# RWKV6 attention and MLP-mixer on one core: another order of the same pieces on the engines

## The chip, the core and the metric

The kernel runs on one core of a Trainium2 chip. The core has five engines with queues of their own: PE (matrix products), DVE and ACT (elementwise work, copies, scans), POOL (elementwise work) and SP, which here only issues DMAs. The 16 DMA engines of the core move data between DRAM and the on-chip memory. Products are summed in PSUM, of which this kernel hands out banks of 128 partitions x 512 numbers. The metric is the device time of one execution in microseconds; lower is better. Before the change three runs took 478.63, 479.74 (the median) and 480.80 us.

## The reference

Four sequences (B = 4) of 768 tokens, 8 heads of 48 numbers. The attention carries a 48 x 48 state for each head from token to token; the mixer then works on the 384 joined numbers of each token, first across tokens (768 to 256 to 768), then across channels (384 to 1536 to 384).

```python
for t in range(S):
    kt, vt, rt, wt = (k[:, :, t], v[:, :, t], r[:, :, t], w[:, :, t])
    cur = np.einsum('bhd,bhe->bhde', u[None] * kt, vt)
    y[:, :, t] = np.einsum('bhd,bhde->bhe', rt, state + cur)
    state = wt[:, :, :, None] * state + np.einsum('bhd,bhe->bhde', kt, vt)
...
x = y.transpose(0, 2, 1, 3).reshape(B, S, H * D)
xt = x.transpose(0, 2, 1)
h = np.maximum(xt @ w_tok1, 0.0) @ w_tok2
u = x + h.transpose(0, 2, 1)
h2 = np.maximum(u @ w_ch1, 0.0) @ w_ch2
return (u + h2).astype(np.float32)
```

## The kernel before

The attention is done in 12 **units** (NU), three to a batch, each 256 tokens of all heads, that is four chunks of T = 64 tokens. Inside a chunk products of keys and queries replace the recurrence; between chunks the state is carried. For a unit i these pieces stand in `attention_pieces(i)`:

- **loads** (`load_rk(i + 1)`, L189): the rows r and k of the *next* unit, four DMAs of 192 KB, keys first. They overwrite a buffer that an earlier unit used.
- **ends** (L452, L456, L457) and **begins** (L464): scans on DVE over the decays w, backwards and forwards. **keys** (L461) and **queries** (L467): DVE scales the rows by them, in place.
- **tokens** (L366): PE turns the scaled keys; **copied** (L371): ACT copies them out of PSUM. **carry** (L386): PE's products of keys and v for the state. **gram** (L336): 64 small products of keys and queries, masked by DVE (L509).
- **scaled** (L522, ACT) and **updates** (L537, DVE): the state chunk by chunk. **before** (L401): products of the queries with the states; **after** (L422): the products within the chunk; **taken** (L428): ACT copies the result into x.
- **w** (L182), **v** (L202), **near** (L207): further loads of the next unit.

A **visit** below means a stretch in which PE takes several of these pieces one behind the other: up to 64 tiny matmuls of 48 or 64 columns in each of before, carry, gram and after.

The mixer is run for each batch. The first batch's (`first_mixing`) has single products: back (L715), turn, up (L964), down (L975), then an add on DVE (L979) into a tile `o`, and its store to the output (L980). The others (`exact_mixing`) add up products of rounded parts ("forms") of both operands: hidden (L684), back (L724), turn (L730), ends and joints (L761 to L768), down (L779 to L781). The forms of the weights are made once, by ACT and DVE (L600 to L622), parts of them are stored to DRAM (L613, L615; tiles `third`), and each of the three later mixings reads these back through a ring of tiles (L647).

**What sets the order.** Each piece is a Python closure that emits instructions for one or more engines. `interleaved(ORDER, ...)` has ten streams of pieces: 0 the products of all mixings, 1 the joints, 2 and 3 the passes that turn the sums into forms for the second products, 4 to 6 the units by i modulo 3, 7 the loads of rows, 8 the conversion and forms of the weights, 9 the second hidden forms. Each digit of the string `ORDER` (L50 to L61) takes the next piece of that stream; 1133 digits in all. `strict()` then ties the instructions on PE, DVE, ACT and SP so that each engine keeps just this order. An engine that meets an instruction whose input isn't there waits, and with it all that is behind. The six PSUM banks are handed out in the order of the table too (`with_banks`). The first 46 us or so, three units of the first batch, stand in a list written by hand ahead of `interleaved`.

Of the kernel before, what the change touches and what calls it, by code (L numbers as in the profile page):

```python
# [47 lines left out]
LEAST, MOST = 2.0 ** -40, 2.0 ** 40  # L48
MID = 3 * G // 4 * SEG1
ORDER = (  # L50
    "888880800080800808008088480884800088040804888000088880448404444848848484880800800888800808040800888444080448888884888800"
    "088888004408474888888080844450588858008850008840000550054588545585845588558454050580555500505508708868800608060608045008"
    "068608566668865656680060688566658668886668908658680608678060888684849606800609488994900840840088000408841401044140440448"
    "008004000000000000040000000044044000000007004040450000000000000004000000005000000005000000000010110055000000005000050004"
    "000500050000000000455547455555555450045555000505600640000000576666666560000000000000000066050006066600066666000666666006"
    "605424655642409062622002020092902329939333340000400044400400001414044100400000400000000000040000000000004444440000000000"
    "740400000500000000000000000050000040500004000010115000500000000005000005500000000050050040455450555055755555055566400006"
    "000506006000660060000054650064000000000065600660606065050066666006600006229666065666202020069220092293939330003230000010"
    "000110000000000000000000000000000000000000000000000000000000000000000000000000000000001001017000000000000000000000000000"
    "00000000000000000000000000000000000000000000000000000"  # L60
)  # L61


# [1248 lines left out]
```

## Time and profile before

| | before |
|---|---|
| median of three runs | 479.74 us (478.63 to 480.80) |
| the profiled execution: time, span | 480.81 us, 479.1 us |
| mean granted clock of PE | 0.995 |
| busy: DVE, ACT, POOL | 338.0, 255.8, 59.8 us |
| moved by DMA | 83.77 MB, 175 GB/s over the span |
| DMA of the rows (L189), issue to landing | median 5.6 us over 36 transfers |

The span is what the profiler recorded from the first to the last instruction; the execution's own time is 1.7 us longer. Three stages follow the hand-written start: the mixing of the first batch with units 3 to 5 of the second (to about 187 us), two mixings beside units 6 to 8 and 9 to 11 (to about 294 and 398 us), and the last mixing. In the views quoted below a row of the timeline has the start and the duration in us, the engine (SPq is a DMA issue on SP), the line, the operation and tiles, how many instructions it joins, and in brackets how long the engine was idle before and for what. A row of the stages has each engine's busy time in that stretch and, in parentheses, its instructions; then the granted clock of PE, the mean busy share of the DMA engines and GB/s.

### The profile page before, as it was taken

The page shows a single profiled execution, that of the slowest core. Times are in us where ns is not written, and L with a number is a line of the kernel's source. Part 1 is how long each engine was busy: PE and PEld are TensorE (multiplying, and loading weights), DVE is VectorE, ACT ScalarE, POOL GpSimd, SP SyncE. Part 2 cuts the span into 40 slices and gives each one's busy share as a digit, 9 for nine tenths or more (in the row PEclk, how much of TensorE's full clock was granted, in tenths as well). Part 3 has the DMA queues.
Part 4 walks back from the last instruction along what each step waited for, and adds up shares of the span by engine and source line. Part 5 has one row for each costly group of instructions (what it writes and reads, how often), then busy time and mean ns, then how long its engine had stood idle before and what let it go on. Part 6 is the DMA issues. An engine that isn't in the chain of part 4 may idle for free.

```text
span 479.1 us, 12687 instructions
## 1 busy us (share of the span) xinstructions
PE 459.6 (96%) x5298; PEld 404.6 (84%) x5298; DVE 338.0 (71%) x478; ACT 255.8 (53%) x588; POOL 59.8 (12%) x58
## 2 busy tenths in 40 slices
PE   3698999999999999999999999999999999999996
PEld 2585588856797668999989979999999979999995
DVE  7999799898787687675588966677596556235341
ACT  6688775765777566341547555251747344033140
POOL 1000000000000001240404001250404003032130
PEclk9989999999999999999999999999999999999999
DMA  8856663765663746764668823394595512336231
GB/s 311 328 187 218 175 214 111 236 217 165 192 185 89 244 144 219 228 190 145 183 219 244 286 79 116 121 269 135 164 262 173 164 49 82 111 106 197 83 101 55
DMA packets 49407, 83.77 MB, mean 175 GB/s; under 512 B 4864, under 2 KB 40576, under 8 KB 49344
## 3 DMA queue, kind: packets, MB, share of 16 engines
q1 hardware_dynamic: 49056, 82.80, 54.8%
q8 instruction: 43, 0.70, 0.6%
q14 instruction: 20, 0.16, 0.1%
q10 hardware_dynamic: 288, 0.10, 0.1%
HBM read 71.87 MB, written 11.01 MB: 173 GB/s over the span
## 4 chain that ended last, share of the span: by engine, by line
PE 92%; DMA 3%; ACT 2%; issue 1%; DVE 1%; SPq 1%; DVEq 0%; ACTq 0%
PE bank L975 10%; PE bank L768 8%; PE bank L761 8%; PE bank L779 8%; PE bank L763 8%; PE bank L781 8%; PE bank L780 8%; PE bank L964 7%; PE bank L684 5%; PE bank L960 3%; PE bank L715 3%; PE bank L336 2%; PE bank L401 2%; PE bank L422 2%; PE kv_ps L386 2%; DMA w<-in_w_dram 2%
## 5 line engine op out<-in xcount | busy, mean ns | idle before, releaser
L754 POOL TENSOR_TENSOR z_high<-z_high 128x384 fp32r<-128x384 f32 x48 | 58.5, 1227 | 403.7 <-DMA ring<-third 187.9
L743 ACT ACTIVATE z_high<-bank 128x384 fp32r<-128x384 f32 x48 | 23.5, 490 | 61.4 <-PE bank L768 61.1
L750 DVE SCALAR_TENSOR_TENSOR z_high<-bank,z_high 128x384 fp32r<-128x384 f32 x48 | 26.4, 553 | 35.0 <-ACT z_high L743 35.0
L522 ACT ACTIVATE before<-state,to_end 112x48 f32<-112x48 f32 x132 | 33.3, 325 | 32.4 <-DVE state L537 20.7
L768 PE MATMUL bank<-z_more,forms 128*128 128x384 f32 x216 | 50.1, 340 | 0.0
L761 PE MATMUL bank<-x_forms,forms 128*128 128x384 f32 x216 | 49.9, 339 | 0.0
L763 PE MATMUL bank<-x_forms,ring 128*128 128x384 f32 x216 | 49.4, 337 | 0.0
L975 PE MATMUL bank<-wch,z 128*128 128x384 f32 x144 | 48.5, 489 | 0.0
L779 PE MATMUL bank<-forms,z_high 128*128 128x384 f32 x140 | 48.2, 344 | 0.0
L787 DVE SCALAR_TENSOR_TENSOR x<-bank,x 128x384 f32<-128x384 f32 x35 | 18.8, 551 | 41.1 <-PE bank L781 41.0
L781 PE MATMUL bank<-forms,z_high 128*128 128x384 f32 x140 | 47.2, 337 | 0.0
L780 PE MATMUL bank<-ring,z_high 128*128 128x384 f32 x140 | 47.1, 337 | 0.0
L975 PEld LDWEIGHTS bank<-wch,z 128*128 128x128 f32 x144 | 26.7, 190 | 17.0
L768 PEld LDWEIGHTS bank<-z_more,forms 128*128 128x128 f32 x216 | 39.0, 188 | 0.0
L761 PEld LDWEIGHTS bank<-x_forms,forms 128*128 128x128 f32 x216 | 38.5, 188 | 0.4
L763 PEld LDWEIGHTS bank<-x_forms,ring 128*128 128x128 f32 x216 | 38.6, 188 | 0.0
L964 PE MATMUL bank<-xT,wch 128*128 128x256 f32 x144 | 31.5, 380 | 0.0
L964 PEld LDWEIGHTS bank<-xT,wch 128*128 128x128 f32 x144 | 27.1, 190 | 3.7
L746 ACT ACTIVATE z_high<-z_high 128x384 fp32r<-128x384 f32 x48 | 25.3, 526 | 3.8 <-ACT z_high L743 0.4
L779 PEld LDWEIGHTS bank<-forms,z_high 128*128 128x128 f32 x140 | 26.3, 188 | 0.3
L780 PEld LDWEIGHTS bank<-ring,z_high 128*128 128x128 f32 x140 | 26.3, 188 | 0.0
L781 PEld LDWEIGHTS bank<-forms,z_high 128*128 128x128 f32 x140 | 26.3, 188 | 0.0
(212 smaller groups left out, 925.6 us busy)
## 6 DMA issues: line engine op xcount, KB each, us to landing
ring<-third SPq DMA_DIRECT2D x144, 192.0 KB, 3.0
raw<-in_w_ch_dram SPq DMA_DIRECT2D x16, 512.0 KB, 4.8
rk<-in_rk_dram SPq DMA_DIRECT2D x36, 192.0 KB, 5.6
near<-in_near_dram SPq DMA_DIRECT2D x8, 768.0 KB, 5.2
w<-in_w_dram SPq DMA_DIRECT2D x10, 520.5 KB, 4.4
vt<-in_v_dram SPq DMA_DIRECT2D x12, 384.0 KB, 4.5
out_dram<-x SPq DMA_DIRECT2D x17, 192.0 KB, 1.9
third<-forms SPq DMA_DIRECT2D x12, 192.0 KB, 3.1
```

Source lines behind the costliest of these rows:

```text
L522: act.mul(t[:ROWS, a], state[bt, g][:ROWS, a], by_last(c, j)[:, a:a + 1])
L746: act.mul(z_form(jt, 2), z_form(jt, 0).bitcast(f32), 1.0 / BASE)
L750: dve.scalar_tensor_tensor(z_form(jt, 1), a, 0.0, z_form(jt, 0).bitcast(f32), op0=ALU.max, op1=ALU.subtract)
L754: pool.tensor_add(z_form(jt, 2), z_form(jt, 2).bitcast(f32), z_form(jt, 1).bitcast(f32))
L761: pe.matmul(a, up[m], xf(0)[:, m], start=m == 0, stop=False)
L763: pe.matmul(a, low[:, m], xf(1)[:, m], start=False, stop=False)
L768: pe.matmul(banks["a", jt], joint, xf(2)[:, m], start=False, stop=m == 2)
L779: pe.matmul(a, z[0], up, start=first, stop=False, skip_group_check=True)
L780: pe.matmul(a, z[1], held[bt, s, half, 1, jt], start=False, stop=False, skip_group_check=True)
L781: pe.matmul(a, z[2], joint, start=False, stop=last, skip_group_check=True)
L964: pe.matmul(ps, now["wch1"][:, m, ts(jt, 128)], xT[:, m, ts(s, SEG)], start=(m == 0), stop=(m == DM // 128 - 1))
L975: pe.matmul(ps, zs[s][:, jt, ts(n, 128)], now["wch2"][:, jt, :], start=(jt == 0), stop=(jt == NJ - 1))
```

## The change

Only the string `ORDER` is replaced. The number of digits of each kind is the same, and within a stream the pieces keep their order, so every engine gets the same instructions with the same operands, in another order between the streams; with it, the PSUM banks fall to other pieces.

```diff
-    "605424655642409062622002020092902329939333340000400044400400001414044100400000400000000000040000000000004444440000000000"
-    "740400000500000000000000000050000040500004000010115000500000000005000005500000000050050040455450555055755555055566400006"
...
+    "966406692296666262422000000440992934332234000332444000700104000110444000000040000000000000000400000044004400400404000000"
+    "000440000400000000000000000005000000000000101010005550000000000000000040005054500500005005545445507550055555555405006400"
```

The first place is SP around the loads of unit 6's rows (`rk_89`, L189 `x4`; the sixth unit uses this buffer), in the first batch's mixing. `out_dram<-o` (L980) are its outputs, `near` is a load of unit 5, `third` parts of the weight forms, `ring` the ring of the next mixing. Before:

```order
L615 DMA third_1_138<-wch_127 128x2x384
L207 DMA near<-in_near_dram 128x1536
L615 DMA third_2_139<-wch_127 128x2x384
L189 DMA rk_89<-in_rk_dram 48x1024 x4
L980 DMA out_dram<-o 128x384 x2
L615 DMA third_3_140<-wch_127 128x2x384
```

and with the change:

```order
L207 DMA near<-in_near_dram 128x1536
L615 DMA third_1_138<-wch_127 128x2x384
L615 DMA third_2_139<-wch_127 128x2x384
L980 DMA out_dram<-o 128x384 x2
L189 DMA rk_89<-in_rk_dram 48x1024 x4
L615 DMA third_3_140<-wch_127 128x2x384
```

The four loads moved from ahead of two output stores to behind them.

The second place is DVE at the same time: the adds that make these outputs (L979), form steps (L604, L619), and unit 6's ends (L452 to L457) and keys (L461). Before:

```order
L604 TENSOR_TENSOR forms_1268<-wch_127,forms_1873 128x768
L979 TENSOR_TENSOR o<-x,bank_884 128x384
L979 TENSOR_TENSOR o<-x,bank_882 128x384
L619 TENSOR_TENSOR forms_1268<-forms_1873,wch_127 128x768
L452 MEMSET starts 112x17
L456 SCALAR_TENSOR_TENSOR to_end_93<-w_90,starts 112x1041
L457 RECIPROCAL starts<-to_end_93 112x16
L461 TENSOR_TENSOR rk_89<-rk_89,to_end_93 112x1024
```

and with the change:

```order
L604 TENSOR_TENSOR forms_1309<-wch_127,forms_1882 128x768
L452 MEMSET starts 112x17
L456 SCALAR_TENSOR_TENSOR to_end_93<-w_90,starts 112x1041
L457 RECIPROCAL starts<-to_end_93 112x16
L979 TENSOR_TENSOR o<-x,bank_886 128x384
L979 TENSOR_TENSOR o<-x,bank_882 128x384
L619 TENSOR_TENSOR forms_1309<-forms_1882,wch_127 128x768
L461 TENSOR_TENSOR rk_89<-rk_89,to_end_93 112x1024
```

The ends moved ahead of both adds. (The scans of L456 and L464 carry the name of the instruction that they are built into; the profile calls them TENSOR_TENSOR_SCAN.)

The third place is SP around the loads of unit 8's rows, at a visit to units 6 and 7 in the second batch's mixing; w, vt and near are other loads of unit 8. Before:

```order
L182 DMA w_90<-in_w_dram 128x1041
L647 DMA ring_2148<-third_4_135 128x384
L189 DMA rk_89<-in_rk_dram 48x1024 x4
L202 DMA vt<-in_v_dram 128x2x384
L207 DMA near<-in_near_dram 128x1536
L647 DMA ring_2024<-third_5_136 128x384 x2
```

and with the change:

```order
L647 DMA ring_2149<-third_4_135 128x384 x2
L182 DMA w_90<-in_w_dram 128x1041
L202 DMA vt<-in_v_dram 128x2x384
L189 DMA rk_89<-in_rk_dram 48x1024 x4
L207 DMA near<-in_near_dram 128x1536
L647 DMA ring_2022<-third_5_136 128x384 x2
```

The rows moved behind vt, which overwrites a tile that unit 6's within-chunk products (L422) read in this visit. On PE the carry of unit 7 (L386) moved ahead of the products of unit 6's queries with the states (L401) in it.

More of the change, by code (lines that the diff above doesn't have):

```diff
@@ L50 @@
 ORDER = (
[L51 to L54, printed above, removed]
@@ L55 @@
-    "000500050000000000455547455555555450045555000505600640000000576666666560000000000000000066050006066600066666000666666006"
-    "605424655642409062622002020092902329939333340000400044400400001414044100400000400000000000040000000000004444440000000000"
-    "740400000500000000000000000050000040500004000010115000500000000005000005500000000050050040455450555055755555055566400006"
-    "000506006000660060000054650064000000000065600660606065050066666006600006229666065666202020069220092293939330003230000010"
@@ L59 @@
-    "000110000000000000000000000000000000000000000000000000000000000000000000000000000000001001017000000000000000000000000000"
-    "00000000000000000000000000000000000000000000000000000"
+    "808888800808800400808084808800080080880044488800488808480008480884888880408884808448080888884804808888400488000484880888"
+    "844440084004444480750000550088888888800005540585880500058885804584584585555458505808055588857058088006080400540066606568"
+    "080860566868668550866666606066086056888686696898860688868455060866798800049408480990488080804488448070044481001100880008"
@@ new lines @@
+    "000000000040000000000400000004400000000440044404000040040004000000000000000000000550000000100011050040000500000000055000"
+    "050005000504500000054544550555055555700554055060404000006005005706006600566060060000000550666060606050666060060566000066"
+    "966406692296666262422000000440992934332234000332444000700104000110444000000040000000000000000400000044004400400404000000"
+    "000440000000400000000000000005000000000000101010005550000000000000000040005054500500005005545445507550055555555405006400"
@@ L61 @@
+    "000606060000000045006000656650000000660656506500066666000066009656660060266600252660200066690022232993923903023030000000"
+    "100110000000000000000000000000000000000000000000000000000000000000000000000000000000000100110000000000000000000000000000"
+    "00000000000000000000000000000000000000000000007000000"
 )
```

## The prediction

> **What bounds the kernel now.** I read the busy times on the page first, then the same by stage, then PE's stretches of 10 us, then PE's waits, and last the timelines around the places that the new table reorders.
>
> ```profile
> PE 459.6 (96%) x5298; PEld 404.6 (84%) x5298; DVE 338.0 (71%) x478; ACT 255.8 (53%) x588; POOL 59.8 (12%) x58
> ```
> ```profile
> core 0: us, PE busy (x) PEld busy (x) DVE busy (x) ACT busy (x) POOL busy (x), PEclk, DMA share, GB/s
> 46.00:60.00 14.00, 13.60 (x50) 8.10 (x51) 10.10 (x14) 10.75 (x16) 0.00 (x0) 1.00 0.68 207
> 60.00:187.00 127.00, 127.00 (x1425) 95.17 (x1424) 106.90 (x137) 84.99 (x180) 0.00 (x0) 1.00 0.57 180
> 187.00:294.00 107.00, 105.88 (x1267) 100.46 (x1266) 78.41 (x117) 53.33 (x132) 20.98 (x16) 1.00 0.63 197
> 294.00:398.00 104.00, 104.00 (x1138) 98.72 (x1137) 70.59 (x110) 49.99 (x125) 21.34 (x16) 1.00 0.52 158
> 398.00:471.00 73.00, 73.00 (x423) 72.93 (x422) 27.50 (x53) 21.59 (x43) 16.21 (x16) 1.00 0.37 112
> ```
> From 60 us to 471 us PE is busy in 127.00 + 105.88 + 104.00 + 73.00 = 409.88 of 411 us, at the full granted clock. The table leaves every piece on PE as it was; it sets only their order. So it cannot shorten what PE does, only the time that PE stands still, and behind the hand-written start (to about 46 us, unchanged) that is 0.40 us in 46 to 60 and 1.12 us in 187 to 294. The waits of PE and its 10-us stretches name the second:
> ```profile
> PE bank L336 <- issue: 1.1, 1, 1.1
> ```
> ```profile
> 230.00:240.00 10.00, 9.75 (x179) 1.00 0.65 180
> 240.00:250.00 10.00, 9.13 (x148) 1.00 0.63 205
> ```
> 0.25 + 0.87 = 1.12 us, one pause. The most that a new order can gain here is therefore 1.1 us, or 1.5 with the 0.40. A measurement of this kernel tells from no change about 0.5%, which is 2.4 us of 479.74: under 477.34 or over 482.14. A gain of that size is out of PE's reach; a loss is not, since any piece that PE, in its fixed order, meets before its input is there costs in full.
>
> **The pause, and what the change does at it (a gain).** PE's timeline at the visit to units 6 and 7:
> ```profile
> 237.53 0.96 PE L401 MATMUL bank<-before,rk 48*64 48x48 f32 x42
> 239.21 0.54 PE L336 MATMUL bank<-rk 48*64 48x64 f32 x21
> 240.87 0.85 PE L336 MATMUL bank<-rk 48*64 48x64 f32 x41 [1.12 <-issue]
> ```
> It stops between two matmuls of one gram, 21 of 62 done, for 1.12 us, and no semaphore is named. What the tiny matmuls of a visit need quickly is instructions: four pieces of up to 64 matmuls, each matmul with its weight load, 42 of them in the first 0.96 us. The DMA views show how they come:
> ```profile
> q8 instruction: 43, 0.70, 0.6%
> ...
> w<-in_w_dram SPq DMA_DIRECT2D x10, 520.5 KB, 4.4
> ```
> ```profile
> DMA packets 496, 1.18 MB, mean 295 GB/s; under 512 B 59, under 2 KB 305, under 8 KB 495
> ...
> q1 hardware_dynamic: 495, 1.17, 97.9%
> q8 instruction: 1, 0.02, 2.3%
> ```
> ```profile
> 232.93 0.32 SPq L647 DMA_DIRECT2D ring<-third  x1
> 233.34 0.39 SPq L182 DMA_DIRECT2D w<-in_w_dram  x1
> 234.49 0.32 SPq L647 DMA_DIRECT2D ring<-third  x1
> 234.86 4.89 SPq L189 DMA_DIRECT2D rk<-in_rk_dram  x4
> ```
> 0.70 MB in 43 packets is 16 KB each. In the whole program PE starts 2 x 5298 matmuls and weight loads, 10596, which is one packet for about 246 of them: a visit eats two. From 234 to 238 the data queue alone held the 16 engines for 97.9%, and one packet ran in there at the end. What filled them is w of unit 8 (520.5 KB), a ring tile (192 KB) and the first two transfers of unit 8's rows (2 x 192 KB): 1.10 MB, close to the 1.17 MB counted. In the new table those rows (L189) stand on SP behind vt of unit 8, and vt can only be overwritten when the within-chunk products (L422) of unit 6 have read it, that is behind the visit. 384 of 1100 KB leave the crush; at the 295 GB/s of the window's row they are 1.3 us of it. So the packet may come up to 1.3 us sooner, and the pause may vanish (1.12 us). Bounds of the gain: nothing, if the packet is late for another reason, and 1.1. I take 0.9, because most of the crush before the packet is gone but w and the ring tiles are still there. The Trainium skill ("Runtime: NRT & Kernel Launch", section "Instruction fetch mechanics") says that instructions come in 16 KiB blocks of 256 over a queue of the engine's own, which the trace bears out (43 packets of 16 KB), and that crossing a block is "mostly hidden". By that sentence the pause would not be a packet and nothing would be gained; the 1.12 us without a semaphore speak against it, and it stands below as rival D.
>
> **Unit 6's rows (a loss).** SP and DVE as they were:
> ```profile
> 159.99 2.41 SPq L189 DMA_DIRECT2D rk<-in_rk_dram  x4
> 165.35 1.66 SPq L980 DMA_DIRECT2D out_dram<-o  x2
> 167.09 6.29 SPq L615 DMA_DIRECT2D third<-wch  x2
> ```
> ```profile
> 162.51 0.96 DVE L604 TENSOR_TENSOR forms<-wch,forms 128x768 fp32r<-128x768 f32 x1 [1.07 <-ACT forms L600]
> ...
> 164.76 0.56 DVE L979 TENSOR_TENSOR o<-x,bank 128x384 f32<-128x384 f32 x1 [1.29 <-PE bank L975]
> 166.05 0.55 DVE L979 TENSOR_TENSOR o<-x,bank 128x384 f32<-128x384 f32 x1 [0.73 <-PE bank L975]
> 167.55 2.33 DVE L456 TENSOR_TENSOR_SCAN to_end<-w,starts 112x1041 f32<-112x1041 f32 x1
> 169.91 0.26 DVE L457 RECIPROCAL starts<-to_end 112x16 f32<-112x16 f32 x1
> 170.08 1.16 DVE L461 TENSOR_TENSOR rk<-rk,to_end 112x1024 f32<-112x1024 f32 x1
> 172.02 2.32 DVE L464 TENSOR_TENSOR_SCAN w<-w,starts 112x1041 f32<-112x1041 f32 x1
> ```
> ```profile
> 163.17 2.85 PE L975 MATMUL bank<-wch,z 128*128 128x384 f32 x8
> 165.95 1.15 PE L422 MATMUL bank<-vt,at 64*64 64x48 f32 x64
> 167.02 7.36 PE L684 MATMUL bank<-x,wtok 128*128 128x384 f32 x22
> 174.22 0.93 PE L366 MATMUL bank<-ident,rk 112*128 112x112 f32 x8
> ```
> The rows were issued at 159.99 and used by DVE at 170.08; the keys were ready at 171.24, 2.98 us before PE turned them (L366) at 174.22. In the new table the four transfers stand behind the two outputs (L980), and SP takes them in order. The outputs wait for their adds on DVE (L979). These wait twice: PE now does the last down-products (L975) behind unit 5's within-chunk products and one hidden product (L684, two matmuls, 7.36 / 11 = 0.67 us), so that they end near 167.75 instead of at 163.17 + 2.85 = 166.02, and DVE now does unit 6's ends (L456, L457) ahead of the adds. My walk along the queues: the form step ahead (L604), one later in its chain than the one quoted, gets its input from ACT near 164.4 and ends near 165.4; ends take 2.33 + 0.26 and a memset, to 168.1; the adds run to 168.6 and 169.1; their outputs go out on SP near 168.65 and 169.15, each with about 0.4 us of issue; the two transfers of keys, which come first of the four, at 169.55 and 169.95. How long they take is the open number:
> ```profile
> L189 SPq DMA_DIRECT2D rk<-in_rk_dram x4: 413/421/423, 195.4 to 196.8; - x4
> ...
> DMA to landing us min/median/max: 3.2/4.5/5.1
> DMA to landing us min/median/max: 5.9/6.0/6.2
> ```
> The first two rows are unit 7's rows, the last unit 6's in the old order, close behind other loads. The new place has the two outputs (384 KB) ahead, and in the old order the engines idled there:
> ```profile
> q1 hardware_dynamic: 336, 0.47, 21.6%
> ```
> That is 168 to 174. So the price lies by the first row: landing after 3.2 to 4.5 us, at 173.2 to 174.5, bounds 173.2 and 176.15 (169.95 + 6.2). The keys take 1.16: ready at 174.4 to 175.7, at the latest 177.3. PE comes to L366 at 174.05 to 174.2 (the same pieces stand ahead of it), so it waits 0.2 to 1.5 us, at most 3.1. I take 0.8. Behind the late keys DVE has the begins (2.32) and a form step (0.94) before the add of the first back-product, whose turn on PE (L730) is three pieces later: another 0.3 us, bounds 0 and 0.5. This place costs 1.1 us (0.2 to 3.6).
>
> **The rest.** The other moves I walked the same way (each queue in its new order, with the durations of the trace): unit 3's ends and keys are earlier, its rows later on SP but in time; the transposes of units 5 and 10, unit 8's products and the banks of the down-products have their input before PE's turn by my walk, though some by only a few tenths; from 385 us on the order is as before. I cost them at nothing. What hides them is the other products that PE has ahead of them; where that cover is short, PE waits out the shortfall, some tenths at such a place. Of the 0.40 us in 46 to 60 I count nothing as won.
>
> **The sum.** The profiled execution took 480.81 us (span 479.1, 1.7 around it), 1.07 above the median 479.74 of the runs shown, 478.63 to 480.8. 480.81 - 0.9 + 1.1 = 481.0 by its own time; by the median 479.74 + 0.2 = 479.9. I name 480.3, between the two and nearer the median, as what is compared is medians.
>
> **The rivals.**
> A, the forecast (0.46): pause gone, rows late by about as much. 479.7 to 481.
> B, pause gone and rows in time (0.19). It needs the keys to land within 3.2 us, as unit 7's fastest did; the 21.6% speak for it. 479.74 - 1.1 = 478.6. It could not be told from no change.
> C, the rows' wait takes over, and it is slower (0.23). One mechanism: SP holds unit 6's rows until the outputs leave, and they land in 5.9 to 6.2 us, as unit 6's did before. PE waits 3.1 us at L366 and 0.5 behind it; with 0.9 won, 479.74 + 2.7 = 482.4. It decides from a landing at about 5.9 us: then 2.4 us net. Against it speaks the empty DMA stretch; for it, that the same rows took 6 us, and that adds 0.3 us late on DVE shift all that follows.
> D, the change doesn't do what it says (0.12): the pause isn't a late packet's, or the packet is as late with the rows gone, since w (520.5 KB) and the ring are still there. Then nothing is won and 1.1 lost: 480.8; with the rows landing late, 483.3.
>
> **How the numbers follow.** Range: B's 478.6 less the runs' half spread would reach 477.6, and C's 482.4 with D's far end 483.3; leaving out a tenth on either side gives 478.3 to 483.0. Faster by over 0.5%: only B with a lucky spread, 0.04. Slower by over 0.5%: two thirds of C (0.16), a third of D (0.04), and 0.06 of A for a place whose slack I have wrong, 0.26. The rest, 0.70, is within 0.5%.
>
> **What would show it.** Right: no wait "issue" of PE at L336 near 240 us, unit 8's L189 issued behind L422 of that visit, PE busy 10.00 there; at 174 us a wait of PE at L366 of 0.2 to 1.5 us for DVE L461, itself waiting for the DMA of rk issued behind L980 near 169.6. Wrong: PE's pause still there with the rows gone (D); L461 starting by 173 (B), or after 175.8 (C); or a wait of PE of over 0.5 us at any other line between 60 and 385 us, which none of my walks gives.

## The result, and the profile after

The changed kernel takes 481.48 us (median of 22 runs, 479.57 to 482.91), the kernel before, on the same chips, 479.55 (22 runs). The ratio is 1.0038, 95% interval 1.0026 to 1.0051: slower by some 1.2 to 2.4 us, a small loss that the runs do tell from nothing, within the bound of 0.5% or at its edge. The profiled execution of the changed kernel took 480.78 us with a span of 479.0 us, 0.7 under its median; that of the kernel before had 480.81, 1.26 over its own. The two spans are therefore alike by chance, and the time has to be looked for stage by stage.

The busy times on the page of the changed kernel, and its stages (columns as before):

```profile
PE 460.9 (96%) x5298; PEld 404.9 (85%) x5298; DVE 340.2 (71%) x478; ACT 254.9 (53%) x588; POOL 56.4 (12%) x58
```
```profile
core 0: us, PE busy (x) PEld busy (x) DVE busy (x) ACT busy (x) POOL busy (x), PEclk, DMA share, GB/s
46.00:60.00 14.00, 13.91 (x54) 8.53 (x53) 11.76 (x17) 11.54 (x17) 0.00 (x0) 1.00 0.75 248
60.00:187.00 127.00, 126.39 (x1420) 93.89 (x1419) 105.83 (x134) 83.34 (x175) 0.00 (x0) 1.00 0.59 178
187.00:294.00 107.00, 107.00 (x1274) 101.64 (x1273) 79.94 (x118) 53.29 (x132) 18.82 (x16) 1.00 0.66 202
294.00:398.00 104.00, 103.05 (x1131) 97.73 (x1130) 71.26 (x109) 50.41 (x127) 20.12 (x16) 1.00 0.48 151
```

Where PE was full before (60 to 187, 294 to 398) it now stands still for 0.61 and 0.95 us, and where it had stood still (187 to 294) it is full. PE's waits between 46 and 470 us in the changed kernel (what it waited for, us in total, times, longest):

```profile
PE bank L336 <- issue: 0.9, 1, 0.9
PE bank L366 <- DVE rk L461: 0.6, 1, 0.6
```

The second is the wait that was forecast. The first reads like the one of before, but it is another: it stands 106 us later. PE's timeline at the visit to units 6 and 7, and then at that to units 9 and 10:

```profile
238.32 0.92 PE L401 MATMUL bank<-before,rk 48*64 48x48 f32 x42
239.20 1.26 PE L336 MATMUL bank<-rk 48*64 48x64 f32 x60
240.25 1.14 PE L422 MATMUL bank<-vt,at 64*64 64x48 f32 x64
...
345.37 0.52 PE L336 MATMUL bank<-rk 48*64 48x64 f32 x17
346.84 0.85 PE L336 MATMUL bank<-rk 48*64 48x64 f32 x42 [0.95 <-issue]
```

The pause near 240 us is gone; an equal one has come up in the next visit of this shape. What leads there on SP, first in the kernel before, then in the changed one:

```profile
335.79 6.98 SPq L647 DMA_DIRECT2D ring<-third  x6
342.86 1.96 SPq L182 DMA_DIRECT2D w<-in_w_dram  x1
```
```profile
332.47 9.02 SPq L647 DMA_DIRECT2D ring<-third  x6
341.58 0.38 SPq L182 DMA_DIRECT2D w<-in_w_dram  x1
```

The load of w for unit 11 (520.5 KB) leaves SP 1.3 us sooner. It used to be issued so late that its data ran behind PE's packet of instructions; now they run ahead of it. Its 128 rows of 4,164 bytes started from 345.44 us on in the kernel before, where PE's packet had started at 343.04; in the changed one they started between 342.69 and 344.49, and the packet at 344.35.

Unit 6's rows on SP, DVE and PE in the changed kernel, with the landing of the four loads:

```profile
167.31 0.83 SPq L980 DMA_DIRECT2D out_dram<-o  x2
168.19 1.84 SPq L189 DMA_DIRECT2D rk<-in_rk_dram  x4
```
```profile
DMA to landing us min/median/max: 3.1/4.1/4.8
```
```profile
166.62 0.26 DVE L457 RECIPROCAL starts<-to_end 112x16 f32<-112x16 f32 x1
166.79 0.95 DVE L979 TENSOR_TENSOR o<-x,bank 128x384 f32<-128x384 f32 x2
167.66 0.95 DVE L619 TENSOR_TENSOR forms<-forms,wch 128x768 fp32r<-128x768 f32 x1
172.53 1.23 DVE L461 TENSOR_TENSOR rk<-rk,to_end 112x1024 f32<-112x1024 f32 x1 [3.92 <-DMA rk<-in_rk_dram]
```
```profile
166.61 6.61 PE L684 MATMUL bank<-x,wtok 128*128 128x384 f32 x20
173.81 0.99 PE L366 MATMUL bank<-ident,rk 112*128 112x112 f32 x8 [0.59 <-DVE rk L461]
```

Each step stands as the prediction had it: ends, adds, stores, rows, a wait of 3.92 us on DVE for them, then one of 0.59 us on PE for the keys.

### The profile page after: what moved, and what is told of

Its sections match the earlier page's. It is cut to its first block, busy times and chain, and to the rows that moved or that the text cites. A ratio compares the mean times of both kernels' runs of the same rounds, so it can differ in the third digit from the quotient of the medians.

```text
span 479.0 us, 12698 instructions
## 1 busy us (share of the span) xinstructions
PE 460.9 (96%) x5298; PEld 404.9 (85%) x5298; DVE 340.2 (71%) x478; ACT 254.9 (53%) x588; POOL 56.4 (12%) x58
## 4 chain that ended last, share of the span: by engine, by line
PE 90%; DVE 3%; DMA 3%; ACT 2%; issue 1%; SPq 0%; DVEq 0%; ACTq 0%
PE bank L975 10%; PE bank L768 8%; PE bank L761 8%; PE bank L779 8%; PE bank L763 8%; PE bank L781 8%; PE bank L780 8%; PE bank L964 7%; PE bank L684 4%; PE bank L960 3%; PE bank L715 3%; PE bank L336 2%; PE bank L401 2%; PE bank L422 2%; PE kv_ps L386 2%; PE bank L724 2%
## 5 line engine op out<-in xcount | busy, mean ns | idle before, releaser
L754 POOL TENSOR_TENSOR z_high<-z_high 128x384 fp32r<-128x384 f32 x48 | 55.2, 1161 | 407.4 <-DVE z_high L750 196.7
L761 PE MATMUL bank<-x_forms,forms 128*128 128x384 f32 x216 | 49.9, 339 | 0.0
L780 PE MATMUL bank<-ring,z_high 128*128 128x384 f32 x140 | 47.1, 337 | 0.0
L761 PEld LDWEIGHTS bank<-x_forms,forms 128*128 128x128 f32 x216 | 38.5, 188 | 0.4
L964 PE MATMUL bank<-xT,wch 128*128 128x256 f32 x144 | 31.7, 380 | 0.0
L780 PEld LDWEIGHTS bank<-ring,z_high 128*128 128x128 f32 x140 | 26.3, 188 | 0.1
## 6 DMA issues: line engine op xcount, KB each, us to landing
w<-in_w_dram SPq DMA_DIRECT2D x10, 520.5 KB, 4.5
```

What stands on the lines that cost most here:

```text
L754: pool.tensor_add(z_form(jt, 2), z_form(jt, 2).bitcast(f32), z_form(jt, 1).bitcast(f32))
L761: pe.matmul(a, up[m], xf(0)[:, m], start=m == 0, stop=False)
L780: pe.matmul(a, z[1], held[bt, s, half, 1, jt], start=False, stop=False, skip_group_check=True)
L964: pe.matmul(ps, now["wch1"][:, m, ts(jt, 128)], xT[:, m, ts(s, SEG)], start=(m == 0), stop=(m == DM // 128 - 1))
```

## The experiments

Two runs are of the unaltered kernels; seven are of one of the two tables with one or two pieces of SP moved and nothing else; three have a wait of SP as well. The move is made in the list of pieces that the table yields, by a pair (piece, the piece behind which it goes):

```diff
+MOVED = (((5, 'loads'), (5, 'seen')), ((10, 'w'), (10, 'v')))
...
-        out = [with_banks(*next(left_of[int(n)])) for n in order]
-        return out
+        taken = {p[0]: p for p in (next(left_of[int(n)]) for n in order)}
+        keys = moved(list(taken), MOVED)
+        return [with_banks(*taken[key]) for key in keys]
```

`moved` takes each first piece out and puts it in again right behind the second. "(5, 'loads')" loads the rows of unit 6, "(10, 'w')" the w of unit 11. Each ratio below is to the kernel before on the same chip.

To read them without the chance of single executions, one table for all, from the starts of PE's matmuls in each profile: the time from the first turn of the first batch (L940) to the last product of L715, near 52 and 397 us; three pieces of that stretch; and two gaps between successive matmuls. Column A goes from the first hidden product of the second batch (the first L684) to the first L761, near 158 to 185 us, and holds unit 6's rows. B goes on from there to the 47th product of L780, near 185 to 245 us, and holds the visit to units 6 and 7. C, from the 73rd to the 144th product of L761, near 294 to 366 us, holds the visit to units 9 and 10. A gap is taken from one start to the next, so it is longer than the wait in the views (1.34 against 1.12 us in the kernel before). The gap at 45 us lies in the hand-written start, ahead of the stretch.

| kernel | stretch | A | B | C | gap in B | gap in C | gap at 45 us | ratio |
|---|---|---|---|---|---|---|---|---|
| before | 343.15 | 28.03 | 59.94 | 72.55 | 1.34 | 0.00 | 1.77 | |
| b_again | 343.07 | 28.03 | 59.66 | 72.52 | 1.06 | 0.00 | 0.02 | |
| b_rows8_late | 341.97 | 28.04 | 58.56 | 72.52 | 0.00 | 0.00 | 0.25 | 0.9991 |
| b_rows8_more | 342.22 | 28.04 | 58.58 | 72.52 | 0.00 | 0.00 | 1.25 | 0.9984 |
| b_rows6_late | 344.04 | 29.21 | 59.38 | 72.52 | 0.78 | 0.00 | 0.67 | 1.0033 |
| b_w11_early | 343.03 | 28.03 | 58.79 | 73.37 | 0.21 | 0.71 | 1.39 | 1.0008 |
| changed | 344.35 | 26.63 | 58.69 | 73.79 | 0.05 | 1.16 | 0.32 | 1.0038 |
| a_again | 344.64 | 26.68 | 58.98 | 73.76 | 0.37 | 1.14 | 1.68 | |
| a_rows6_early | 343.42 | 25.45 | 58.72 | 74.03 | 0.07 | 1.40 | 0.32 | 1.0003 |
| a_w11_late | 345.46 | 26.49 | 58.97 | 74.77 | 0.32 | 0.00 | 0.32 | 1.0013 |
| a_both | 342.69 | 25.45 | 59.40 | 72.58 | 0.78 | 0.00 | 0.32 | 0.9997 |
| a_fixed | 342.29 | 25.45 | 58.99 | 72.62 | 0.36 | 0.00 | 0.32 | 0.9989 |
| a_fixed_start | 342.65 | 25.45 | 59.31 | 72.59 | 0.68 | 0.00 | 0.32 | 0.9982 |
| b_best | 341.97 | 28.04 | 58.56 | 72.52 | 0.00 | 0.00 | 0.32 | 0.9960 |

(In A the two tables put different products between its ends, so that only kernels of one table are compared there. At 45 us a matmul of that line takes 0.32 by itself.)

**b_again: the kernel before, once more.**

> The kernel before, unaltered, profiled once more. Theory (a pause of PE is a packet of instructions that comes late behind data): the pause of 1.1 us at L336 near 240 us comes back, since unit 8's rows fill the DMA engines ahead of its packet in every execution; the pause of 1.3 us at L918 near 45 us, in the hand-written start that the change leaves alone, was chance of that one execution and is gone or shorter. Rival (both are fixed waits of the program): both come back within 0.1 us.

One run, 479.25 us. The pause near 240 us is there, 0.8 us by the waits; that at 45 us isn't (0.02). So the first has a standing cause, though its size moves, and the second comes and goes. The execution profiled at first was unlucky in a part that the change leaves alone, and that is why the two spans agreed.

**b_rows8_late and b_rows8_more: only the rows of unit 8 behind the visit.**

```diff
+MOVED = (((7, 'loads'), (7, 'v')),)
```

> The kernel before with one move on SP: unit 8's rows behind unit 8's vt, as in the change. Theory: the pause at L336 near 240 us is gone (0.1 us or less) and nothing else alters, 0.9 to 1.2 us faster, ratio 0.9975 to 0.9982. Rival (the pause belongs to the visit, or to carry standing behind before on PE): the pause stays at 1.1 us, ratio 1.000.

> The kernel before with unit 8's rows behind unit 8's vt, once more, for a narrower interval beside b_best on the same chip. Theory: no pause near 240 us, ratio 0.9975 to 0.9995. Rival: a pause of 0.5 us or more there in this execution, ratio 1.000.

0.9991 (0.9978 to 1.0005) and 0.9984 (0.9964 to 1.0005). The first lies over the range that was expected for it, and the times alone don't settle it, since both intervals take in 1. The profiles do: no gap at the place in either, B 1.1 to 1.4 us shorter than in the two profiles of the kernel before, A and C the same within 0.03 us. In the old table this move alone is worth what that part of the change was thought to be. One smaller pause, 0.2 us, stands at the visit near 152 us in the second.

**b_rows6_late: only the rows of unit 6 behind the output stores.**

```diff
+MOVED = (((5, 'loads'), ('down', 2, 1, 10)),)
```

> The kernel before with one move on SP: unit 6's rows behind the two output stores, as in the change, but DVE and PE in the old order, so that the stores leave near 165.4 and 166.6 us. Theory: rows issued from about 167 us, landing 3.1 to 4.8 later; the keys start near 171 instead of 170.1, PE still has about 2 us left at L366: no wait, ratio 1.000 within 0.001. The cost in the change would then need DVE's and PE's new order as well. Rival (the move on SP alone costs what the change lost there): PE waits 0.5 us or more at L366, ratio 1.001 to 1.002.

1.0033 (1.002 to 1.0046), and A 1.18 us longer. The theory's "no wait" was wrong. The rival had the loss, but not its place, and 1.0033 lies over the 1.002 that it allowed. DVE, ACT and PE in this kernel:

```profile
170.91 1.23 DVE L461 TENSOR_TENSOR rk<-rk,to_end 112x1024 f32<-112x1024 f32 x1 [2.19 <-DMA rk<-in_rk_dram]
172.05 0.95 DVE L604 TENSOR_TENSOR forms<-wch,forms 128x768 fp32r<-128x768 f32 x1
```
```profile
173.03 0.84 ACT L607 ACTIVATE wch<-forms 128x768 f32<-128x768 f32 x1 [2.78 <-DVE forms L604]
173.78 0.85 ACT L686 ACTIVATE h<-bank 128x384 f32<-128x384 f32 x2
```
```profile
172.77 0.93 PE L366 MATMUL bank<-ident,rk 112*128 112x112 f32 x8
174.69 2.85 PE L724 MATMUL bank<-h,wtok 128*128 128x384 f32 x8 [0.98 <-ACT h L686]
```

The keys were ready in time for L366, as expected. But DVE waited 2.19 us for the rows, and behind the keys in its queue stood a form step (L604); ACT waited for that form (L607), and behind it in ACT's queue stood the copies of the hidden products (L686), for which PE waited 0.98 us at L724. The late rows cost PE a microsecond over two queues that have nothing to do with them. The reserve at the piece that reads the rows (from their being ready to their use), 2.98 us before, was the wrong one to read.

**b_w11_early: w of unit 11 ahead of the last ring load.**

```diff
+MOVED = (((10, 'w'), (2, ('ends', 1, 4))),)
```

> The kernel before with one move on SP: w of unit 11 ahead of the last ring load before the visit to units 9 and 10 instead of behind it, so that it is issued near 341.3 us instead of 342.9, as in the change. Theory: its data run when PE's packet is asked for, the packet starts 0.5 to 1.3 us later than before and a pause of 0.3 to 1.2 us appears at L336 near 346 us, 1.0006 to 1.0025. Rival (the new pause comes from the new order on PE, the carry ahead of the products with the states): no pause there, ratio 1.000.

1.0008 (0.9982 to 1.0034): 1 and the whole range of the theory lie in the interval, so the times can't tell. The profile can. SP, and PE at the place:

```profile
340.68 0.38 SPq L182 DMA_DIRECT2D w<-in_w_dram  x1
341.85 0.32 SPq L647 DMA_DIRECT2D ring<-third  x1
```
```profile
345.03 0.64 PE L336 MATMUL bank<-rk 48*64 48x64 f32 x28
346.17 0.73 PE L336 MATMUL bank<-rk 48*64 48x64 f32 x33 [0.50 <-issue]
```

In none of the six other profiles of the old table is there a gap here; with that one move, and PE's order as before, there is one of 0.71. Here the rows of w started between 341.76 and 343.78 us, and PE's packet at 343.94. So the new pause comes from where w stands on SP, and the carry ahead of the products with the states isn't needed for it. That the pause in B was only 0.21 in this execution shows again how its size moves.

**a_again: the changed kernel, once more.**

> The changed kernel, unaltered, profiled once more. Theory: PE waits 0.5 to 0.8 us at L366 near 173 us for unit 6's keys, pauses 0.8 to 1.2 us at L336 near 346 us with no semaphore named, and not near 240 us. Rival (the pauses fall where they will): one of them is missing, or another of 0.5 us stands elsewhere behind 60 us.

One run, 483.12 us. L366 waits 0.6 us, the pause in C is there (1.14), that in B is a third of what it was (0.37), and the one at 45 us struck here (1.68).

**a_rows6_early: the rows of unit 6 ahead of the stores again.**

```diff
+MOVED = (((5, 'loads'), (5, 'seen')),)
```

> The changed kernel with one move on SP: unit 6's rows ahead of the two output stores again. Theory: the keys are done before 170 us, the wait at L366 is gone and with it what followed on DVE, 0.7 to 1.2 us less than the change, ratio to the kernel before 1.0013 to 1.0024 where the change has 1.0038. Rival (the rows weren't what PE waited for there, DVE's order was): the wait stays at 0.5 us or more, ratio 1.0033 to 1.0043.

1.0003 (0.9985 to 1.0021), still lower than the theory's 1.0013, which its interval takes in. The wait at L366 is gone, A is 1.18 us shorter (0.81 of it up to the first L724, 0.37 behind it), and the pause in C stays, as nothing was done about it.

**a_w11_late, a_both and a_fixed: w of unit 11 behind the visit, alone and with the former; then held by a wait.**

```diff
+MOVED = (((10, 'w'), (10, 'v')),)
...
+MOVED = (((5, 'loads'), (5, 'seen')), ((10, 'w'), (10, 'v')))
...
+MOVED = (((5, 'loads'), (5, 'seen')), ((10, 'w'), (10, 'gram')))
+GATED = {(10, 'w'): (10, 'carry')}
```

(GATED lets the first DMA of a piece wait for the last instruction of another.)

> The changed kernel with one move on SP: w of unit 11 behind vt of unit 11, that is behind the visit to units 9 and 10. Theory: the packet starts by 343.3 us instead of 344.35, the pause of 0.95 us at L336 is gone, w lands by 354 us, before DVE needs it at 353.8 or a few tenths late with no wait of PE; 0.9 to 1.3 us less than the change, ratio 1.0011 to 1.0020. Rival (new order on PE): the pause stays, ratio 1.0033 to 1.0043.

> The changed kernel with both moves. Theory: both gone, and PE stands still nowhere for over 0.4 us from 60 us to 470 us; 1.7 to 2.4 us less than the change, ratio to the kernel before 0.9988 to 1.0003, and behind 60 us its profile is 1.0 to 1.3 us shorter than that of the kernel before, by the pause near 240 us. Rival (a pause goes on to the next visit, as it did in the change): another pause of 0.5 us or more, ratio 1.002 or more.

> The changed kernel with unit 6's rows ahead of the two output stores, and w of unit 11 held on SP until PE has done unit 10's carry, which is within the visit to units 9 and 10 and behind the point at which the packet is asked for. Theory: the packet starts by 343.5 us, w is issued near 344.7 and lands by 352, before the ends of unit 11 need it; no wait of PE at L336 near 346, none at L366 near 173 and near 361. From the first turn of the first batch to the last instruction of PE the profile counts 342.2 to 342.9 us (343.4 before, 344.6 changed); ratio 0.9975 to 1.000. Rival (packets late at random, whatever stands ahead of them): a pause of 0.5 us or more near 346.

a_w11_late has 1.0013 (0.9991 to 1.0034), and its profiled execution doesn't bear out what was expected: the pause in C is gone, but C got longer still, by 0.98 us. (That execution took 482.20 us, 1.07 over the median of its kernel, so the loss needn't be in all of them; the ratio itself lies in the range that was expected.) DVE and PE there, and the landing of w in it and in a_both:

```profile
356.04 2.33 DVE L456 TENSOR_TENSOR_SCAN to_end<-w,starts 112x1041 f32<-112x1041 f32 x1 [3.08 <-DMA w<-in_w_dram]
```
```profile
362.93 0.60 PE L366 MATMUL bank<-ident,rk 112*128 112x112 f32 x4 [1.32 <-DVE z_high L750]
```
```profile
DMA to landing us min/median/max: 7.5/7.5/7.5
```
```profile
DMA to landing us min/median/max: 4.5/4.5/4.5
```

Behind vt and with the rows on its heels, the same load took 7.5 us in the execution of a_w11_late and 4.5 in that of a_both, which had no wait there. Late w holds unit 11's ends, and the passes behind them in DVE's queue that empty the banks for PE. a_both has 0.9997 (0.9977 to 1.0016), in the range that was expected, but with a gap of 0.78 in B (a wait of 0.6) where the first profile of the changed kernel has none; so the expectation of no pause over 0.4 us was not met. a_fixed has 0.9989 (0.9967 to 1.0011): w issued at 343.66, landing 3.9 us later; both losses are gone and no wait of PE is listed from 40 us on. Its stretch of 342.29 is 0.8 us shorter than that of the kernel before.

**b_best and a_fixed_start: the start as well.**

The pause at 45 us, in both kernels alike, is of the same kind. In the start, w and v of unit 3 and the next raw weights were issued from 40 us on, just ahead of the packet. Both kernels hold them on SP until PE has done unit 2's products with the states, near 42 us:

```diff
-           behind(t2[3], lambda: load_w(3)), p2, product1, e2["mask"], lambda: load_v(UB), behind(e2["own_gram"], to_ch[1][0]), e2["before"], h[4],
+           p2, product1, e2["mask"], e2["before"], behind(e2["before"], lambda: load_w(3)), lambda: load_v(UB), to_ch[1][0], h[4],
```

b_best adds to this only the move of b_rows8_late; a_fixed_start is a_fixed with this start.

> The kernel before with unit 8's rows behind unit 8's vt, and in the hand-written start w and v of unit 3 and the next raw weights held on SP until PE has done unit 2's products with the states, near 42 us, so that the packet asked for near 41.6 us meets an empty queue. Theory: no pause at L918 near 45 us and none at L336 near 240; the profile counts 342.2 to 342.6 us from the first turn to PE's end; the times scatter less and their median is 0.6 to 1.4 us under that of the kernel before, ratio 0.997 to 0.9987. Rival (the late raw weights hold up ACT's and DVE's conversion instead): PE waits 0.5 us or more between 46 and 60 us, ratio 1.000 or more.

> The kernel of a_fixed with the start of b_best: w and v of unit 3 and the next raw weights held until PE has done unit 2's products with the states. Theory (the two tables differ by their late rows and late packets alone): the same time as b_best within 0.15%, ratio to the kernel before 0.995 to 0.998, and the stretch from the first turn to the verdict 342.2 to 342.7 us. Rival (something else in the new table costs or gains): more than 0.2% from b_best's 0.996, ratio over 0.998 or under 0.994.

b_best takes 478.31 us against 479.78 of the kernel before, 0.996 (0.9939 to 0.9982): faster than both kernels, though by little, and by slightly more than was expected. b_rows8_more, which lacks only the new start, took 479.36 on the same chip. PE's busy time in its stages:

```profile
44.00:60.00 16.00, 16.00 (x61) 1.00 0.88 278
60.00:187.00 127.00, 126.99 (x1426) 1.00 0.58 180
187.00:294.00 107.00, 107.00 (x1275) 1.00 0.64 194
294.00:394.00 100.00, 100.00 (x1114) 1.00 0.53 162
```

PE stands still for 0.01 of 350 us. The times scatter less too: 477.46 to 479.28 in 12 runs, against 478.30 to 484.72 in 29.

a_fixed_start has 0.9982 (0.9965 to 1.0000), 0.22% behind b_best and so just past the rival's mark, but the intervals overlap, and the times leave it unclear. Its stretch is 0.68 us longer, and B alone is 0.75 longer, with a gap of 0.68; C agrees within 0.1 us, and A can't be compared. What is left against the new table is thus the pause in B, which it makes shorter and doesn't end.

All 14 traces together point to the reason: how long ahead of the visit's first product a load of 384 KB or more leaves SP. (Single ring loads of 192 KB stand among them in every kernel.)

| visit, load | us ahead of the visit | profiles | gap, us |
|---|---|---|---|
| units 6 and 7, old table: rows of unit 8 | 2.7 | 4 | 0.21 to 1.34 |
| the same, rows behind the visit: w of unit 8 | 4.2 | 3 | 0.00 |
| units 6 and 7, new table: w of unit 8 | 2.6 | 7 | 0.05 to 0.78 |
| units 9 and 10, old table: w of unit 11 | 1.1 | 6 | 0.00 |
| the same, b_w11_early | 2.7 | 1 | 0.71 |
| units 9 and 10, new table: w of unit 11 | 2.1 | 3 | 1.14 to 1.40 |
| the same, w within or behind the visit | - | 4 | 0.00 |

The new table takes the rows of unit 8 away from the visit, but puts w of unit 8 behind one more ring load, 1.6 us nearer to it. That this alone leaves the pause was not tried by itself.

## Why the pauses are packets of instructions

The prediction argued this from a pause without a semaphore and a late packet. The runs show it in three ways.

**They stop at one place in the program's length.** Count what the profile records on PE (matmuls, weight loads and the few other instructions) up to each pause. The pauses without a semaphore of 0.1 us and more from 42 us on stand at 1985, 5825 or 8385, and the small ones near 152 us (waits of 0.1 and 0.2 us, in two profiles) at 4033: that is 7, 22, 32 and 15 times 256, and 193 more, whatever instruction is there. The packets hold 16 KB, and 43 of them serve some 10,711 recorded instructions, about 250 each.

**They follow the packet.** When it is on time, the packet needed at 8385 starts when PE has begun 31.6 to 31.7 times 256 instructions, about 1.1 packets ahead. The starts of the packets needed at 1985, 5825 and 8385 in all 14 profiles, in units of 256, with the gap:

| needed at | started at (gap, us) |
|---|---|
| 1985 | 6.8 to 7.2 (0.02 to 0.32); 7.31 (0.67); 7.59 (1.25); 7.66 (1.39); 7.74 (1.68, 1.77) |
| 5825 | 21.67 and 21.68 (0.00); 21.70 (0.05 to 0.37); 21.73 (0.36, 0.78); 21.77 (1.06); 21.82 (1.34); 21.96 (0.78); 22.00 (0.68) |
| 8385 | 31.6 to 31.7 (0.00); 31.89 (0.71); 32.15 (1.16); 32.20 (1.14); 32.34 (1.40) |

The later the packet, the longer the gap, but for the last two of 5825, which started late in the count and whose transfers took only 0.9 us, where those ahead of them took up to 1.48. Where PE waited over 0.4 us, it went on 1.2 to 1.5 us after the packet's own transfer had ended.

**They come and go with data ahead of the packet.** b_rows8_late takes away 384 KB and the gap in B goes; b_w11_early puts 520.5 KB ahead of one more ring load and a gap comes in C; a_fixed holds them and it goes; b_best does the same in the start. There the pause also comes and goes by itself (0.32 us or less, a matmul's own time, in seven of the twelve profiles with the old start), so what speaks for the start is b_best's times more than its profile; a_fixed_start, 0.9982, against a_fixed, 0.9989, doesn't tell. No other part of the kernel was touched in these, b_best's start aside.

By the sentence of the Trainium skill that was weighed in the prediction ("Runtime: NRT & Kernel Launch", section "Instruction fetch mechanics"), crossing a block costs little that shows. That agrees with most of the 43 packets here, and not with those that are needed within or just behind a visit while data hold the queues: up to 1.3 us by PE's waits.

## Why the prediction was right, and where not

- **PE as the bound, no gain beyond 1.5 us:** held. Even b_best, in which PE doesn't stand still, has a median 1.47 us lower (0.4% by the ratio), and part of that comes from the start, which the change leaves alone.
- **The pause near 240 us, gain 0.9, bounds 0 and 1.1:** held in cause, less so in size. (When it came, 23 of the gram's 64 products were done, not 21 of 62: two rows that lie between those shown have one more each.) In the two profiles of each unaltered kernel B went from 59.94 and 59.66 to 58.69 and 58.98, 0.97 us on average. But four profiles have the old order at this visit and seven the new, and over all of these B went from 59.44 to 59.01, 0.43 us. The new table doesn't end the pause: five of its seven profiles have 0.3 to 0.8 there. The reason that the prediction gave for taking less than all, that w and the ring are still there, is what remains.
- **Unit 6's rows, cost 1.1, of it 0.8 at L366 and 0.3 behind:** held. By a_rows6_early it is 1.18, 0.81 up to the first L724 and 0.37 behind it; the wait listed at L366 itself is 0.6. The walk had the keys' rows issued at 169.55, and they were at 168.19 in an execution that ran 1.2 us ahead of the first from the start; the landing of 3.1 to 4.8 us lay by the row that was chosen.
- **"The rest ... I cost them at nothing":** this is the step that failed. The visit to units 9 and 10 now pauses as that to units 6 and 7 had, 1.24 us of C in either pair of profiles. The walk followed that visit's operands, which are in time; it did not ask what SP issues ahead of the visit's packet, although that very argument was made for the visit 106 us earlier. The forecast's own test, a wait of over 0.5 us at another place, points to it.
- **The sum:** +0.2 us was forecast; with the missing 1.2 it is +1.4, and the stretch of the table gives 1.39 (344.35 and 344.64 against 343.15 and 343.07). The medians differ by 1.93. With the 0.43 of all profiles for the gain, the three pieces make 1.18 + 1.24 - 0.43 = 2.0, an estimate from few executions each; the interval of the ratio, 1.2 to 2.4 us, takes in both. The chance of the pause at 45 us may add either way.
- **The forecast time, 480.3, and its mechanism of two effects that cancel (rival A):** the time came out 1.2 us over it, by that third effect. It lies outside A's own 479.7 to 481; that it is within the whole range is owed to the room left for slower cases, which had other reasons, and so to luck.
- **The rivals:** B's (rows in time) and C's (rows landing after 5.9 us) did not come. Of D, the doubt that the pause is a packet's was refuted by b_rows8_late and the counts above; its other half, a packet late by w and the ring with the rows gone, came in part.

## What to carry to other kernels

A tuned kernel whose bound engine is busy to 99.7% (409.88 of 411 us here) has only its stalls left to win; ask of each whether its engine waited for data or for its own instructions. Short instructions by the hundred eat a packet in a few microseconds (a visit's four pieces, 512 instructions, took 3.7 us in b_rows8_late): look at what transfers are asked for ahead of such a stretch, in every one of them. Here loads of 384 KB and more issued 2.1 to 2.7 us ahead went with pauses, and those issued 4.2 or 1.1 us ahead, or within or behind it, did not. And when a load gets later, walk on from the instruction that waits through everything queued behind it on that engine and on the next; the reserve at the reader alone says little.

## What was not expected of the hardware

PE's packets of 16 KB at the three places took 0.92 to 1.85 us, and how full the data queue was doesn't sort them: 0.96 us at 44.20 in the kernel before, where data filled most of the engines' time, and up to 1.28 with next to no data beside them. What went with the long gaps was a late start: up to about a packet's length of instructions later than it might (7.74 where 6.8 to 7.2 is on time). Such starts make executions differ with no change of the program: the pause at 45 us was 1.8, 0.0, 0.3, 1.3, 0.7 and 1.4 us in the six profiles of the kernel before and of it with one move, which are alike up to that point; the first two are of the same kernel, and so are the third and the fourth. And a load of 520.5 KB, issued at the same place of two kernels that are alike around it, landed after 4.5 us in one execution and 7.5 in the other.
